# Decode attention on one core: keys and values in loads of head pairs, scores summed by identity matmuls, values on four column strips

## The chip, the cores and the metric

The kernel runs on one core of a Trainium2 chip. The metric is device time in microseconds, the median of several executions. One further execution is taken with the hardware profiler; its own span (first to last instruction) is what the views of the profile divide up.

## The reference

One token (a row of 640 numbers) passes a conditioned transformer block: a modulation from `c`, a layer norm, attention over a cache, a second layer norm, and a gated feed-forward layer. Cut to what matters:

```python
# x: 1 x 640, k_cache and v_cache: 32 heads x 16384 x 128, all bf16
mod = (silu(c) @ w_mod)                      # six vectors of 640: sa, ca, ga, sb, cb, gb
h = layernorm(x) * (1 + ca) + sa
q = (h @ wq)                                 # 32 heads x 128
scores = einsum('hd,hkd->hk', q, k_cache) * 128 ** -0.5
p = softmax(scores)
o = einsum('hk,hkd->hd', p, v_cache)
x = x + ga * (o.reshape(1, 4096) @ wo)
h = layernorm(x) * (1 + cb) + sb
x = x + gb * ((silu(h @ w_gate) * (h @ w_up)) @ w_down)
```

Each head has one query only, so every key and every value is read once and used once. Keys and values are 268.4 MB of the 290.5 MB that the kernel reads.

## The kernel before

The program is a list of operations. Each one names its engine, a position `pos` in time, the operations that it depends on, and a function that issues it. `emit` sorts each engine's operations by position and writes them out one after another, with a semaphore wait in front of an operation where a dependency asks for one. So the order on each engine and on each DMA queue is what the positions say. All large loads are issued from SyncE's queue (SP) in that order; a load that waits holds up those behind it.

The start: `w_mod` (4.9 MB), `w_q` (5.2 MB) and the keys of heads 0 and 1 are issued at once, head 0 in four pieces; `c` and `x` come as columns over the 128 partitions, 10 bytes each, on ScalarE's queue. TensorE makes the modulation and then `q`, every head's row copied onto all partitions (`qbc`, L337).

Then, head by head, with 128 positions of the cache on each of 128 partitions:

- Keys. `kring` has two buffers of one head (32 KB a partition). VectorE multiplies the whole buffer by the query (L414), adds the upper half of each row of 128 to the lower half (L416), folds twice more to 32 and 16 columns (L423), sums the last 16 (L426), and takes the maximum of the 128 scores of each partition (L429).
- Softmax. GpSimd reduces the maximum over the partitions (L432). ScalarE makes the exponentials (L436) with the sum of each partition. GpSimd sums those over the partitions (L439), and ScalarE makes the reciprocal through Ln and Exp (L441, L443).
- Values. `vring` has two buffers of one head. TensorE multiplies them, four positions at a time: the stationary operand is 128 x 4 exponentials, the moving operand 128 x 512 values, 32 matmuls a head, into 4 x 512 of PSUM (L453). ScalarE copies that out (L459), and four fp32 matmuls pick the four diagonal blocks and add them (`diag`, L466). For the last head, whose values come in three pieces, the values are the stationary operand (L477).
- The results are laid out for the output projection (L487 to L496).

The key load of head h + 1 waits for the sum L426 of head h - 1, and the value load of head h waits for the value matmuls of head h - 2; they alternate on SP.

The end: `w_o` is loaded ahead of the last values, `w_gate`, `w_up` and `w_down` follow into the key buffers once these are free. Behind the last values come the projection (L519), a layer norm of six small steps on three engines (L283 to L295), the gate and up matmuls (L562), the down matmuls (L580), and the store.

Of the kernel before, what the change touches and what calls it, by code (L numbers as in the profile page):

```python
# [21 lines left out]
class _Op:  # L22
    __slots__ = ("eng", "pos", "fn", "deps", "chan", "val", "name", "seq", "sig")

    def __init__(self, eng, pos, fn, deps, name, seq, chan=None):
        self.eng = eng
        self.pos = pos
        self.fn = fn
        self.deps = [d for d in deps if d is not None]
        self.name = name  # L30
        self.seq = seq
        self.chan = chan
        self.val = None
        self.sig = False


class _Plan:

    ENGS = ("sp", "act", "dve", "pe", "pool")

    def __init__(self, nc, es):
        self.nc = nc
        self.es = es
        self.ops = []
        self.chans = {}
        for e in self.ENGS:
            if e == "sp":
                continue
            self.chans[e] = _Chan(es.enter_context(nc.semaphore("ch_" + e)), 1)
        self.dma_chans = {}  # L50
        self.names = None
# [7 lines left out]
    def op(self, eng, pos, fn, deps=(), name=""):  # L59
        o = _Op(eng, pos, fn, list(deps), name, len(self.ops))  # L60
        self.ops.append(o)
        return o

    def dma(self, pos, out_ap, in_ap, slot_key, deps=(), name="", eng="sp", noncontig=False):
        nc = self.nc

        def fn(e, out_ap=out_ap, in_ap=in_ap, noncontig=noncontig):
            if noncontig:
                with nc.allow_non_contiguous_dma(reason="tiny vector layout change"):
                    return e.dma_start(out_ap, in_ap)  # L70
            return e.dma_start(out_ap, in_ap)

        o = _Op(eng, pos, fn, list(deps), name, len(self.ops), chan=self.dma_chan(slot_key))
        o.sig = True
        self.ops.append(o)
        return o

    def emit(self, block):
        nc = self.nc
        bad = []  # L80
        for o in self.ops:
            for d in o.deps:
                d.sig = True
                if not ((d.pos, d.seq) < (o.pos, o.seq)):
                    bad.append("%s(%s@%.2f) depends on later %s(%s@%.2f)" % (o.name, o.eng, o.pos, d.name, d.eng, d.pos))
        assert not bad, "plan order violates dependencies:\n" + "\n".join(bad[:40])
        per_eng = {e: [] for e in self.ENGS}
        for o in self.ops:
            per_eng[o.eng].append(o)
        for e in self.ENGS:  # L90
            per_eng[e].sort(key=lambda o: (o.pos, o.seq))
# [6 lines left out]
        self.per_eng = per_eng  # L98

        def run(eng_name, eng):  # L100
            known = {}
            for o in per_eng[eng_name]:
                need = {}
                for d in o.deps:
                    assert d.val is not None, (o.name, d.name)
                    k = id(d.chan)
                    if k not in need or need[k][1] < d.val:
                        need[k] = (d.chan, d.val)
                for k, (ch, v) in need.items():
                    if known.get(k, 0) >= v:  # L110
                        continue
                    eng.wait_ge(ch.sem, v)
                    known[k] = v
                ins = o.fn(eng)
                if ins is not None and self.names is not None:
                    self.names[ins.ins.name] = o.name
                if o.sig:
                    assert ins is not None, o.name
                    ins.then_inc(o.chan.sem, o.chan.inc)
# [21 lines left out]

def build(nc, A_x, A_k, A_v, A_wq, A_wo, B_wg, B_wu, B_wd, c_in, w_mod, out):
# [3 lines left out]
    assert Dh == 128 and D % 128 == 0 and S % 128 == 0  # L146
    KC = D // 128
    TT = S // 128
    NF = F // 128
    FR = F - 128 * NF  # L150
    FCH = NF + (1 if FR else 0)
    GQ = 4

    GROUPS = [(0, 8), (8, 8), (16, 8), (24, 4), (28, 4)]
    assert H % GQ == 0 and all(128 % n == 0 for _, n in GROUPS) and GROUPS[-1][0] + GROUPS[-1][1] == H
    SCALE = float(Dh) ** -0.5
    EPS = 1e-5
    PERIOD = 19.8
    NKP0 = 4

    def TK(h):
        return 20.0 + PERIOD * h

    es = ExitStack()
    with es:
        block = es.enter_context(nc.Block())
        plan = _Plan(nc, es)

        def sb(name, shape, dtype):
            return es.enter_context(nc.sbuf_tensor(name, list(shape), dtype))  # L170

        WM_E = KC * 6 * D
        WQ_E = KC * H * 128
        FFN_E = 2 * KC * F + FCH * D
        VEX = 10240
        wreg = sb("wreg", [128, max(WM_E, H * D)], BF16)
        wm_v = wreg[:, 0:WM_E].rearrange("p (k n) -> p k n", k=KC)
        wo_v = wreg[:, 0:H * D].rearrange("p (k n) -> p k n", k=H)  # L180
        kring = sb("kring", [128, 2, TT, 128], BF16)
        vbig = sb("vbig", [128, 2 * TT * 128 + VEX], BF16)
        vring = vbig[:, 0:2 * TT * 128].rearrange("p (s t d) -> p s t d", s=2, t=TT)
        assert WQ_E - VEX <= TT * 128
        wq_v = vbig[:, 2 * TT * 128 + VEX - WQ_E:2 * TT * 128 + VEX].rearrange("p (k n) -> p k n", k=KC)
        assert FFN_E <= 2 * TT * 128
        kflat = kring[:].rearrange("p s t d -> p (s t d)")
        wg_v = kflat[:, 0:KC * F].rearrange("p (k n) -> p k n", k=KC)
        wu_v = kflat[:, KC * F:2 * KC * F].rearrange("p (k n) -> p k n", k=KC)
        wd_v = kflat[:, 2 * KC * F:2 * KC * F + FCH * D].rearrange("p (k n) -> p k n", k=FCH)  # L190
        acc_sb = sb("acc_sb", [4, 2, 512], F32)
        ident_f = sb("ident_f", [4, 4], F32)
        qbc = sb("qbc", [128, H, 128], BF16)
        S_sb = sb("S_sb", [128, 2, TT], F32)
        P_sb = sb("P_sb", [128, 2, TT], BF16)
        ones_f = sb("ones_f", [128, 128], F32)
        ones_bf = sb("ones_bf", [128, 128], BF16)
        ident = sb("ident", [128, 128], BF16)
        msk = {n: sb("msk%d" % n, [128, 128 // n], F32) for n in sorted({n for _, n in GROUPS})}
        e8 = {n: sb("e%d" % n, [128, n], BF16) for n in sorted({n for _, n in GROUPS})}  # L200
        Z = sb("Z", [128, len(GROUPS), 128], BF16)
        A_sb = sb("A_sb", [128, H], BF16)
        c_col = sb("c_col", [128, KC], BF16)
        x_col = sb("x_col", [128, KC], BF16)
        pm = sb("pm", [128, H], F32)
        gm = sb("gm", [128, H], F32)
        nb = sb("nb", [128, H], F32)
        rs = sb("rs", [128, H], F32)
        Ls = sb("Ls", [128, H], F32)
        lnl = sb("lnl", [128, H], F32)  # L210
        rl = sb("rl", [128, H], F32)
        on_f = sb("on_f", [128, H], F32)
        warm = sb("warm", [128, 2], F32)
# [4 lines left out]
        rr = sb("rr", [128, KC], F32)  # L218
        silu_c = sb("silu_c", [128, KC], BF16)
# [22 lines left out]
        q_ps = [psb[0], psb[1]]  # L242
        OT_ps = psb[2]
        attn_ps = psb[3]
        mod_ps = psb[4]
        A_ps = psb[5]
        st_ps = psb[6]
        f_ps = psb[7]
        acc_ps = [psb[0], psb[1]]
        g_ps = psb[0]  # L250
        u_ps = psb[1]

        POOL, ACT, DVE, PE = "pool", "act", "dve", "pe"
        op = plan.op


        o_onesf = op(DVE, 0.0, lambda e: e.memset(ones_f[:], 1.0), name="ones_f")
        o_ones = op(POOL, 0.0, lambda e: e.memset(ones_bf[:], 1.0), name="ones")
        o_ident = op(POOL, 0.1, lambda e: e.affine_select(
            out=ident[:], in_=ones_bf[:], pattern=[[1, 128]], compare_op=ALU.is_equal,  # L260
            fill=0.0, base=0, channel_multiplier=-1), deps=[o_ones], name="ident")
        o_wz = op(DVE, 0.1, lambda e: e.memset(warm[:], 1.0), name="warm0")
        op(POOL, 0.2, lambda e: e.partition_all_reduce(
            warm[:, 1:2], warm[:, 0:1], channels=128, reduce_op=bass.bass_isa.ReduceOp.max), deps=[o_wz], name="warm")
# [4 lines left out]
        d_c = plan.dma(0.0, c_col[:], c_in[0].rearrange("(p k) -> p k", p=128), "c", name="dma_c", eng="act")  # L269
        d_x = plan.dma(0.01, x_col[:], A_x[0, 0].rearrange("(p k) -> p k", p=128), "x", name="dma_x", eng="act")  # L270
        d_wm = plan.dma(0.0, wm_v, wm_src, "wm", name="dma_wmod")
        d_wq = plan.dma(0.1, wq_v, wq_src, "wq", name="dma_wq")


        op(ACT, 0.05, lambda e: e.preload_act_table_set("natural_log_exp_and_others"), name="tbl")
        o_ec = op(ACT, 0.2, lambda e: e.activation(out=ec[:], in_=c_col[:], func=ACTF.Exp, scale=-1.0), deps=[d_c], name="ec")  # L276
# [360 lines left out]
```

## Time and profile before

| | us |
|---|---|
| Median of the 3 runs | 693.13 (692.8 to 693.34) |
| Span of the profiled execution | 690.5 |
| VectorE busy | 616.9 (89%) |
| GpSimd busy | 381.3 (55%) |
| TensorE busy, matmuls | 361.5 (52%) |
| ScalarE busy | 81.1 (12%) |
| DMA packets of SP's queue, share of 16 engines | 98.4% |
| Mean granted TensorE clock | 0.722 of full speed |

Busy time is the time in which an engine executes an instruction; the share is that of the span. DMA shares are the time of the packets over 16 DMA engines; a packet is one contiguous row, 32 KB for keys and values here. A line such as L414 is line 414 of the kernel. In the list of groups, `out<-in` gives the tiles, then partitions x elements, the count, the busy time, the mean of one, and the idle time in front with what ended it.

### The profile page before, as it was taken

Reading aid. Unit: us, or ns where it says so; the run is one execution under the profiler, and the core shown is the slowest. Engines: PE = TensorE matmul, PEld = TensorE weight load, DVE = VectorE, ACT = ScalarE, POOL = GpSimd, SP = SyncE. Lnnn points to the kernel's source line nnn. Section 1 sums busy time; section 2 is a strip of 40 time slices with the busy share of each in tenths; the row PEclk is TensorE's granted clock in tenths of the full one; section 3 lists DMA queues with packets and bytes.
Section 4 is the critical chain, followed back from the end, with each engine's and each line's share of the span. In section 5 each row is a group of like instructions: output and inputs, shape, how many; then the busy total and the mean of one; then the engine's idle time right before and its main releaser. Section 6 shows DMA issues by size and latency. Waiting matters only on the chain.

```text
span 690.5 us, 4719 instructions
## 1 busy us (share of the span) xinstructions
PE 361.5 (52%) x1940; PEld 159.6 (23%) x1941; DVE 616.9 (89%) x226; ACT 81.1 (12%) x284; POOL 381.3 (55%) x71
## 2 busy tenths in 40 slices
PE   0275055665445455565545445556544544656577
PEld 0242022221112122222112112222111212222176
DVE  0099999999999999999999999999999999999900
ACT  0021001111011111111011110111101111111110
POOL 0005565555777666555677656555577766655500
PEclk9987567667766767767777776766776776676655
DMA  9999999999999999999999999999999999999994
GB/s 382 404 436 400 416 427 427 429 431 433 427 432 433 429 435 426 437 429 432 431 433 427 433 435 429 432 431 431 432 433 427 431 432 435 433 425 430 420 426 177
DMA packets 12150, 290.78 MB, mean 421 GB/s; under 512 B 1696, under 2 KB 1760, under 8 KB 2400
## 3 DMA queue, kind: packets, MB, share of 16 engines
q1 hardware_dynamic: 11840, 290.48, 98.4%
q8 instruction: 15, 0.25, 0.1%
q10 hardware_dynamic: 288, 0.00, 0.0%
q14 instruction: 7, 0.06, 0.0%
HBM read 290.47 MB, written 0.00 MB: 421 GB/s over the span
## 4 chain that ended last, share of the span: by engine, by line
DVE 89%; DMA 7%; PE 2%; issue 1%; ACT 0%; ACTq 0%; DVEq 0%; SPq 0%
DVE kring L414 40%; DVE kring L416 21%; DVE kring L423 16%; DVE S_sb L426 11%; DMA x_col<-in_A_x_dram 4%; DMA kring<-in_B_w_up_dram 3%; DVE pm L429 1%; PE psb L562 1%; PE psb L580 0%; PE psb L311 0%; PE psb L333 0%; ACT qbc L337 0%; PE psb L283 0%; PE psb L290 0%; DVE e L396 0%
## 5 line engine op out<-in xcount | busy, mean ns | idle before, releaser
L453 PE MATMUL psb<-vbig,P_sb 128*4 128x512 bf16 x992 | 286.8, 460 | 263.3 <-ACT P_sb L436 244.9
L432 POOL PARTITION_ALL_REDUCE gm<-pm x32 | 262.3, 8198 | 226.7 <-DVE pm L429 226.7
L414 DVE TENSOR_TENSOR kring<-kring,qbc 128x16384 bf16<-128x16384 bf16 (+1 forms) x35 | 278.3, 7950 | 3.2 <-ACT qbc L337 3.2
L453 PEld LDWEIGHTS psb<-vbig,P_sb 128*4 128x4 bf16 x992 | 94.8, 98 | 442.2 <-ACT P_sb L436 265.9
L416 DVE TENSOR_TENSOR kring<-kring 128x8192 bf16<-128x8192 bf16 (+1 forms) x35 | 142.1, 4059 | 1.2
L439 POOL PARTITION_ALL_REDUCE Ls<-rs x32 | 117.9, 3683 | 29.7 <-ACT P_sb L436 29.7
L423 DVE TENSOR_TENSOR kring<-kring 128x4096 bf16<-128x4096 bf16 x64 | 112.5, 1758 | 2.2
L426 DVE TENSOR_REDUCE S_sb<-kring 128x128 f32<-128x2048 bf16 x32 | 73.1, 2286 | 1.1
L466 PE MATMUL psb<-ident_f,acc_sb 4*128 4x1 f32 x248 | 32.5, 248 | 23.8 <-ACT acc_sb L459 23.8
L459 ACT ACTIVATE acc_sb<-psb,rl 4x512 f32<-4x512 f32 x31 | 21.0, 678 | 155.4 <-PE psb L453 155.3
L466 PEld LDWEIGHTS psb<-ident_f,acc_sb 4*128 4x128 f32 x248 | 29.8, 186 | 39.5 <-ACT acc_sb L459 39.5
L434 ACT ACTIVATE nb<-gm 128x1 f32<-128x1 f32 x32 | 6.5, 202 | 222.7 <-POOL gm L432 222.7
L441 ACT ACTIVATE lnl<-Ls 128x1 f32<-128x1 f32 x32 | 6.5, 203 | 121.8 <-POOL Ls L439 121.8
L283 PE MATMUL psb<-st,ones_f 128*128 128x1 f32 x4 | 1.2, 362 | 29.0 <-ACT x_f L300 28.4
L540 DVE TENSOR_TENSOR tt<-attn_bf,modb 128x5 f32<-128x5 bf16 x1 | 0.2, 166 | 14.7 <-ACT attn_bf L539 14.7
L277 DVE TENSOR_SCALAR dd<-ec 128x5 f32<-128x5 f32 x1 | 0.2, 172 | 14.7 <-ACT ec L276 14.7
L436 ACT ACTIVATE P_sb<-S_sb,nb 128x128 bf16<-128x128 f32 x32 | 12.9, 402 | 1.2
L285 DVE SCALAR_TENSOR_TENSOR xc<-x_f,psb 128x5 f32<-128x5 f32 x1 | 0.2, 161 | 12.6 <-PE psb L283 12.6
L333 PE MATMUL psb<-vbig,h_col 128*128 128x512 bf16 x39 | 10.4, 434 | 0.9 <-DVE h_col L319 0.9
L429 DVE TENSOR_REDUCE pm<-S_sb 128x1 f32<-128x128 f32 x32 | 9.2, 286 | 1.1
L490 ACT ACTIVATE Z<-msk,on_f 128x16 bf16<-128x16 f32 (+1 forms) x32 | 10.0, 311 | 1.1
L562 PE MATMUL psb<-h_col,kring 128*128 128x1 bf16 (+1 forms) x140 | 8.8, 199 | 1.2 <-DVE h_col L549 1.0
(63 smaller groups left out, 91.2 us busy)
## 6 DMA issues: line engine op xcount, KB each, us to landing
kring<-in_A_k_cache_dram SPq DMA_DIRECT2D x31, 4096.0 KB, 16.5
vbig<-in_A_v_cache_dram SPq DMA_DIRECT2D x31, 4096.0 KB, 25.7
vbig<-in_A_wq_dram SPq DMA_DIRECT2D x1, 5120.0 KB, 26.6
wreg<-in_w_mod_dram SPq DMA_DIRECT2D x1, 4800.0 KB, 14.5
kring<-in_A_k_cache_dram SPq DMA_DIRECT2D x4, 1024.0 KB, 31.5
wreg<-in_A_wo_dram SPq DMA_DIRECT2D x1, 3840.0 KB, 37.7
kring<-in_B_w_gate_dram SPq DMA_DIRECT2D x1, 2160.0 KB, 18.5
kring<-in_B_w_up_dram SPq DMA_DIRECT2D x1, 2160.0 KB, 23.8
```

The lines of the kernel that those rows point to most:

```text
L414: o_m = op(DVE, base + 3.3 * c, lambda e, ksl=ksl, qb=qb: e.tensor_tensor(out=ksl, in0=ksl, in1=qb, op=ALU.mult), deps=[d_k[h][c], o_qbc[h ...
L416: fd.append(op(DVE, base + 3.3 * c + 2.2 + (6.6 if npc == 1 else 0.0), lambda e, ksl=ksl: e.tensor_tensor(out=ksl[:, :, 0:64], in0=ksl[:, ...
L423: prev = [op(DVE, base + 15.5 + 1.5 * i, lambda e, kslot=kslot, w=w: e.tensor_tensor(out=kslot[:, :, 0:w], in0=kslot[:, :, 0:w], in1=kslot ...
L426: o_red[h] = op(DVE, base + 18.2, lambda e, s2=s2, kslot=kslot, w=w: e.tensor_reduce(out=S_sb[:, s2], in_=kslot[:, :, 0:w], axis=AX.X, op= ...
L429: o_max = op(DVE, base + 18.5, lambda e, h=h, s2=s2: e.tensor_reduce(out=pm[:, h:h + 1], in_=S_sb[:, s2], axis=AX.X, op=ALU.max), deps=[o_ ...
L432: o_gm = op(POOL, base + 19.0, lambda e, h=h: e.partition_all_reduce(gm[:, h:h + 1], pm[:, h:h + 1], channels=128, reduce_op=bass.bass_isa ...
L436: o_exp[h] = op(ACT, base + 19.4, lambda e, h=h, s2=s2: e.activation(out=P_sb[:, s2], in_=S_sb[:, s2], func=ACTF.Exp, scale=SCALE, bias=nb ...
L439: o_L = op(POOL, base + 20.0, lambda e, h=h: e.partition_all_reduce(Ls[:, h:h + 1], rs[:, h:h + 1], channels=128, reduce_op=bass.bass_isa. ...
L453: last = e.matmul(acc_ps[s2][0:4, :], lhsT=P_sb[:, s2, 4 * c:4 * c + 4], rhs=vring[:, s2, 4 * c:4 * c + 4, :].rearrange("p t d -> p (t d)" ...
L459: o_acc[h] = op(ACT, base + 28.6, lambda e, h=h, s2=s2: e.activation(out=acc_sb[:, s2], in_=acc_ps[s2][0:4, :], func=ACTF.Copy, scale=rl[0 ...
L466: last = e.matmul(OT_ps[:, h:h + 1], lhsT=acc_sb[:, s2, 128 * i:128 * (i + 1)], rhs=ident_f[:, i:i + 1], start=(i == 0), stop=(i == 3))
L562: last = e.matmul(ps_t[0:w, j:j + 1], lhsT=wv[:, k, cols], rhs=h2_col[:, k:k + 1], start=(k == 0), stop=(k == KC - 1))
```

## The change

The body is rewritten. What changes in what is done:

- Two heads are worked on together, 64 partitions each. A load brings the keys (or values) of a pair: 8.39 MB, 256 positions or 64 KB contiguous on each partition. Keys have two buffers of a pair; values have one buffer of a pair, so the values of pair p wait for the value matmuls of pair p - 1.
- VectorE multiplies by the query and folds once, from 128 columns to 64, in two halves (32 of the 64 remaining columns each). The remaining sum of 64 is made on TensorE: 64 matmuls with the identity as the stationary operand accumulate in PSUM; the moving operand takes one column of all 256 positions, a step of 128 elements.
- The maximum over the partitions of a head: VectorE takes each partition's maximum from PSUM, ScalarE spreads it over a diagonal, a matmul with a block matrix of ones brings all of a head's values to each of its partitions, and VectorE takes the minimum (signs are turned). The sums of the exponentials are added up once, at the end, by one matmul.
- The values of a pair are 64 matmuls of 512 columns with 128 x 8 exponentials (those of the other head are zero); they go to four column strips of the array in turn, each with its own 32 partitions of PSUM.
- On TensorE the order in step p is: first half of the sums, values of pair p - 1, second half of the sums, `diag` of pair p - 1, the matmul of the maximum.
- `w_mod` lies in the second key buffer at first, `w_q` in the value buffer, `w_o` comes into the first key buffer ahead of the last values, the feed-forward weights into the second. `c` and `x` come as rows and are turned by matmuls. The chunks of the feed-forward layer are taken with a step of four columns, `w_up` comes in two parts.
- Operations have no position any more; each engine runs them in the order in which they are listed. The planner can write a loop, but `LOOP_ON` is empty, so all is written out.

```diff
-        kring = sb("kring", [128, 2, TT, 128], BF16)
-        vbig = sb("vbig", [128, 2 * TT * 128 + VEX], BF16)
+        kring = sb("kring", [128, 2, T2, 128], BF16)
+        vbuf = sb("vbuf", [128, T2, 128], BF16)
...
-        kv = lambda t, h: t[0, h].rearrange("(p t) d -> p t d", p=128)
+        k_src = lambda p: A_k[0, 2 * p:2 * p + 2].rearrange("h (q t) d -> (h q) t d", q=64)
+        v_src = lambda p: A_v[0, 2 * p:2 * p + 2].rearrange("h (q t) d -> (h q) t d", q=64)
...
+        def load_k(p):
+            deps = [o_R[p - 2]] if p >= 2 else ([o_mod] if p == 1 else [])
+            d_k[p] = dma(kring[:, p % 2], k_src(p), ("k", p % 2), deps=deps, name="dma_k%d" % p)
+
+        def load_v(p):
+            deps = [o_pv[p - 1]] if p >= 1 else [o_q[-1]]
+            cuts = VCUT if p == NP - 1 else [0, T2]
+            d_v[p] = [dma(vbuf[:, a:b, :], v_src(p)[:, a:b, :], ("v", c), deps=deps, name="dma_v%d_%d" % (p, c))
+                      for c, (a, b) in enumerate(zip(cuts, cuts[1:]))]
+
+        def pv(p):
...
+                    for j in range(a // 4, b // 4):
+                        s = j % 4
+                        last = e.matmul(acc_ps[32 * s:32 * s + 8, :], lhsT=PZ[:, p % 2, j, :],
+                                        rhs=vbuf[:, 4 * j:4 * j + 4, :].rearrange("p t d -> p (t d)"),
+                                        start=(j < 4), stop=(j >= NCH - 4), tile_position=(0, 32 * s))
...
+        def diag(p):
+            def f_diag(e):
+                last = None
+                for i in range(4):
+                    last = e.matmul(OT_ps[:, 0:2], lhsT=acc_sb[:, 128 * i:128 * (i + 1)], rhs=sel[:, i:8:4],
+                                    start=(i == 0), stop=(i == 3))
...
+        def reduce_mm(p, c, fold):
+            def f_R(e):
+                last = None
+                for d in range(QW * c, QW * c + QW):
+                    last = e.matmul(S_ps[p % 2][:, 0:T2], lhsT=ident[:], rhs=kring[:, p % 2, :, d],
+                                    start=(d == 0), stop=(d == 63))
+                return last
...
+        def fold(p, c):
+            kv4 = kring[:, p % 2].rearrange("p t (a d) -> p t a d", a=2)[:, :, :, QW * c:QW * c + QW]
...
+            o_m = op(DVE, lambda e: e.tensor_tensor(out=kv4, in0=kv4, in1=q4, op=ALU.mult),
+                     deps=[d_k[p]] + o_qev[p // 2], name="mult%d_%d" % (p, c))
+            return op(DVE, lambda e: e.tensor_tensor(out=kv4[:, :, 0], in0=kv4[:, :, 0], in1=kv4[:, :, 1], op=ALU.add),
+                      deps=[o_m], name="fold%d_%d" % (p, c))
+
+        def step(p):
+            f0 = fold(p, 0)
+            r0 = reduce_mm(p, 0, f0)
+            if p >= 1:
+                pv(p - 1)
+            f1 = fold(p, 1)
+            o_R[p] = reduce_mm(p, 1, f1)
+            if p >= 1:
+                diag(p - 1)
+            o_pm = op(DVE, lambda e: e.tensor_reduce(
+                out=pm[:, p:p + 1], in_=S_ps[p % 2][:, 0:T2], axis=AX.X, op=ALU.max), deps=[o_R[p]], name="pm%d" % p)
+            o_d2 = op(ACT, lambda e: e.activation(out=d2[:], in_=negid[:], func=ACTF.Copy, scale=pm[:, p:p + 1]),
+                      deps=[o_pm, o_negid], name="d2_%d" % p)
+            o_mx = op(PE, lambda e: e.matmul(mx_ps[:, 0:64], lhsT=bd_f[:], rhs=d2[:], start=True, stop=True),
...
+            o_nb[p] = op(DVE, lambda e: e.tensor_reduce(
+                out=nb[:, p:p + 1], in_=mx_ps[:, 0:64], axis=AX.X, op=ALU.min), deps=[o_mx], name="nb%d" % p)
...
         load_k(0)
         load_k(1)
+        load_v(0)
+        step(0)
+        load_k(2)
+        step(1)
+        load_v(1)
...
+        for p in range(2, NP):
+            plan.in_loop(LOOP_ON, "pairs", (p - 2) // 2, NLOOP)
+            if p + 1 < NP:
+                load_k(p + 1)
...
+            step(p)
+            load_v(p)
```

## The prediction

> **What bounds the kernel now.** I read the page's slices and chain first, then how long each key load takes to land, then the instruction groups, then the first 75 and the last 60 us of the timeline. Slices and chain:
>
> ```profile
> DVE  0099999999999999999999999999999999999900
> ...
> DMA  9999999999999999999999999999999999999994
> ...
> DVE 89%; DMA 7%; PE 2%; issue 1%; ACT 0%; ACTq 0%; DVEq 0%; SPq 0%
> ```
>
> VectorE and the DMA engines are both full from slice 2 to 38; the chain names VectorE because it never waits. Whether the DMA has anything to spare shows in the time from issue to landing of the key load of one head, near 110 us and near 616 us (two answers of the DMA view, a line of each):
>
> ```profile
> kring<-in_A_k_cache_dram SPq DMA_DIRECT2D x1, 4096.0 KB, 13.2
> ```
>
> ```profile
> kring<-in_A_k_cache_dram SPq DMA_DIRECT2D x1, 4096.0 KB, 19.6
> ```
>
> It is issued when VectorE frees its buffer, once per head; 6.4 us more over some 26 heads means that a head's 8.39 MB takes about 0.25 us longer than VectorE's 19.28 us (start to start of L414 in the chain, 596.73 to 616.01). So the DMA is the slower of the two, at about 19.5 us a head, and VectorE lives off a shrinking lead. Whatever VectorE is spared, the steady part cannot get shorter than the bytes. The groups (busy, mean ns, idle before):
>
> ```profile
> L453 PE MATMUL psb<-vbig,P_sb 128*4 128x512 bf16 x992 | 286.8, 460 | 263.3 <-ACT P_sb L436 244.9 <-DMA vbig<-in_A_v_cache_dram 18.4
> L414 DVE TENSOR_TENSOR kring<-kring,qbc 128x16384 bf16<-128x16384 bf16 x31 | 269.1, 8681 | 0.0
> L416 DVE TENSOR_TENSOR kring<-kring 128x8192 bf16<-128x8192 bf16 x31 | 137.2, 4425 | 1.1
> L423 DVE TENSOR_TENSOR kring<-kring 128x4096 bf16<-128x4096 bf16 x32 | 73.3, 2292 | 1.1
> L426 DVE TENSOR_REDUCE S_sb<-kring 128x128 f32<-128x2048 bf16 x32 | 73.1, 2286 | 1.1
> ```
>
> TensorE's pace is read from one burst of 32 value matmuls cut in two (busy and count, granted clock, DMA share, GB/s):
>
> ```profile
> 57.70:60.60 2.90, 2.90 (x7) 0.50 0.84 362
> 60.60:66.00 5.40, 5.40 (x26) 1.00 1.06 452
> ```
>
> A burst starts at half clock, 0.42 us per 512 columns, and goes on at 0.21. Over all heads (286.8 us / 31 = 9.25 us a burst) some 11 of 32 run cold, 4.8 us. The end of the kernel:
>
> ```profile
> 667.36 1.01 PE L477 MATMUL psb<-P_sb,vbig 128*128 128x1 bf16 x32 [1.42 <-DMA vbig<-in_A_v_cache_dram]
> ...
> 673.98 4.42 PE L562 MATMUL psb<-h_col,kring 128*128 128x1 bf16 x70 [1.05 <-DVE h_col L549]
> ...
> 678.59 4.40 PE L562 MATMUL psb<-h_col,kring 128*128 128x1 bf16 x70 [0.19 <-DMA kring<-in_B_w_up_dram]
> ...
> 683.33 3.12 PE L580 MATMUL psb<-gu_col,kring 64*128 64x1 bf16 x60 [0.34 <-DVE gu_col L571]
> ```
>
> The last values land at 667.3, and 23.2 us of single-file work follow to 690.5. So the time is: when the last value bytes land, plus that tail. I cost the change in these two terms.
>
> **VectorE and TensorE per pair of heads.** Removed: two folds at L423 (2.29 and 1.23 us), the sum at L426 (2.29) and the maximum per head, and all GpSimd reductions (L432, L439). Left: per half of a pair one multiply of 16,384 (8.68) and one fold of 8,192 (4.43): 13.1 us, 26.2 a pair against 38.6. The runs are 32 long instead of 128; the folds with runs of 64, 32 and 16 all cost 0.16 us over 1.92 elements per ns, so the run length is free. Added on TensorE: 64 matmuls of 256 columns (R, two halves of 32), reading one element in every 256 B. No row has such a moving operand. By columns alone a half costs 32 x 0.21 = 6.8 us at half clock and 3.5 at full. Nearest rows for a stride: weight loads with a one-column matmul at clock 0.50, 31 ns contiguous (L477), 52 with a step of 10 B (L580, 70 in 3.8 us), 63 with 26 B (L562). That is 126 ns per 256 strided elements, under the 213 of a cold matmul (no loss); taken as a ratio it doubles a half, to 13.6 us. I take 6.8: the bursts start after 7 us or more of idle TensorE, hence cold, and the nearest count stays under it.
>
> The Trainium skill ("SBUF — State Buffer", Specifications) speaks against this: lines are 16 bytes, and full bandwidth needs at least two hits in each; R has one. It gives no factor; L580 and L562 agree in direction (52 and 63 ns).
>
> Values: 64 matmuls of 512 columns a pair, on four column strips. Bounds: all four at once, 16 x 0.216 = 3.5 us; one after another, 13.8 (both warm, since R's first half runs just ahead). No row has two strips. I take 3.5, because the strips share neither array columns nor PSUM partitions, and L477 issues a matmul every 31 ns, so 64 of them need only 2.0 us of issue. The skill ("TensorE: Matmul & The Clock Gate", Part 3) reports 2.38x for three strips; with 3x it would be 4.6 us and the sum 1.1 later.
>
> The softmax step waits on TensorE: VectorE's maximum of 256 from PSUM (0.4, from 0.29 for 128), a scale on ScalarE (0.2), an fp32 matmul (0.7, from 0.59 at L283), a minimum (0.2), hand-overs: 1.8 us; with the four `diag` matmuls (1.05, L466) and their copy queued ahead, 2.7. VectorE idles through R's second half and this, its next multiply standing behind `nb`. A pair takes 26.2 + 6.8 + 2.7 = 35.7 us, with R's first half and the values (10.3) under the second multiply and fold (13.1). The DMA needs 38.8. So the steady part stays the DMA's: nothing gained or lost but its bytes' pace, and 3 us a pair of cover.
>
> **Descriptors.** Packets in the trace: 8 KB 309 ns, 32 KB 1,215, 40 KB 1,514: about 8 ns fixed each. A 64-KB row saves one, and a semaphore write per load goes: 8 x 8 + 9 = 73 ns for each of 32 loads, -2.3 us. Bounds: 0 if rows are cut in two; a loss is unlikely, as rate rises with size (26.5, 27.0, 27.1 B/ns).
>
> **Head of the kernel.** The key load after the start found the queue empty before, 13.3 us to land instead of 9.7 (first line of the DMA view of 55.5 to 56.5 us); that gap and the next one cost 2.0 us. After: w_q lands at 27.8 as now; key pair 0 19.4 later, 47.2 (VectorE starts 11.6 us later than its 35.7 now, covered by its shorter pairs). Keys 1, values 0, keys 2, values 1 could follow without a gap until 124.8. But with one value buffer, values 1 wait for pv of pair 0, which stands on TensorE behind R's first half of pair 1: 47.3 + 26.2 + 6.8 + 1.8 = 82.1, + 13.1 + 6.8 + 3.5 = 105.5 to issue, + 19.4 + 3.6 (empty queue) = 128.5. Gap 3.8, so +1.8. Bounds: at 3.5 a half no gap, -2.0; at 13.6, +15.5. Later value loads wait the same way but are issued some 6 us before the queue empties (pair 2: about 140 against 146). The key loads stand in front of them on SP and wait for R of two pairs earlier, which is done first. In the last pair w_o is put ahead of the last values and covers their wait by 6 us.
>
> **Tail.** Last quarter of the last values, 16 matmuls: 0.9 to 1.8 against 1.05. Then, against 1.1 us from values to w_o now: a copy from PSUM (0.7), `diag` 1.1, three VectorE or ScalarE steps and one matmul (1.1): +1.9. Gate and up read weights 8 B apart instead of 26: 70 x 52 ns instead of 63, -0.8 each, and up no longer waits 0.2. Sum +0.6, from 0 to +1.5. Gone from the chip altogether: GpSimd's 381 us, off the path, worth nothing.
>
> **Sum.** 690.5 - 2.3 + 1.8 + 0.6 = 690.6. The runs shown have a median 2.6 above the profiled span, so 693.2: no change (a difference under 0.2%, 1.4 us, can't be told from none).
>
> **Rivals.**
> 1. *The head gap closes*: R warm from the start (3.5 a half). 690.5 - 2.3 - 2.0 + 0.3 = 686.5, 689 measured. For: the clock turned in 2.9 us in the burst shown. Against: 4.8 on average, and 7 us of idle ahead.
> 2. *Strided reads bind* (slower). With every element at half the full rate a half is 0.42 x 11 + 0.21 x 21 = 9.3 us: head gap 8.8, 695.6, 698 measured, the pair at 38.2 still hidden. This is the place where the skill's line rule would bite. From 9.8 us a half (306 ns a matmul) the pair passes 38.8 and every pair pays: at 13.6 a pair is 13.1 + 13.6 + 3.5 + 13.6 + 2.7 = 46.5, 7.7 x 14 pairs more, near 800. For: 63 against 31 ns. Against: both are below what a matmul of 256 needs.
> 3. *Strips run one after another* (13.8): values 1 issued 10.3 later in the head; pairs at 13.1 + 6.8 + 13.8 + 3.5 + 2.7 = 39.9, barely over; pv of pair 14 outruns w_o's cover by 7; last quarter +3. 690.6 + 20 = 711, 713 measured. For: nothing in the trace overlaps two matmuls. Against: the disjoint strips.
> 4. *64-KB rows are cut in two*: +2.3, 695.5; inside the forecast's range. A loop cannot slip in: `LOOP_ON` is empty.
>
> **How the numbers follow.** Forecast 0.48, its own range 689.5 to 697; rival 1 0.17, rival 2 0.22 (half of it above 705), rival 3 0.13. Faster: rival 1 and 0.13 of the forecast, 0.30. Same 0.17. Slower: 0.18 of the forecast with rivals 2 and 3, 0.53. The range 689 to 714 leaves out the worst of rival 2.
>
> **What would show it.** R's halves at 5.8 to 6.8 us and clock 0.5 to 1.0 in them; value bursts of 3.5 to 5; VectorE waiting for key loads from pair 4 on, 26.2 busy of 38.8; 64-KB packets near 2,420 ns; values 1 landing at 127 to 129 us; the last values near 665 to 668 and 23.5 to 24.5 us behind them. Wrong if VectorE waits for TensorE in the middle pairs, or if the loads stand idle there.

## The result and the profile after

The changed kernel takes 870.73 us (median of 4 runs, 869.71 to 871.27) against 693.1 for the kernel before (4 runs on the same chip): a ratio of 1.2561, with a 95% interval of 1.2543 to 1.2579. The prediction was 693.2 us with a range of 689 to 714. The profiled execution has a span of 869.2 us, against 690.5 before, and a mean granted TensorE clock of 0.585, against 0.722.

The slices of the changed kernel (busy tenths in 40 slices of the span; `PEclk` is the granted clock) and the first line of its chain of waits:

```profile
DVE  1083836539091745729092654819183562909211
...
PEclk9955565555656565565656565565656555565655
DMA  9998939597894959598694959689594959777492
...
PE 68%; DVE 25%; DMA 5%; ACT 1%; issue 1%; SPq 0%; DVEq 0%
```

Neither VectorE nor the DMA is full any more, and the chain runs through TensorE for 68% of the time (2% before). The DMA view of 300 to 400 us, in 2.5-us slices, shows what became of the resource that bounded the kernel before. Twice it stands still for four slices, some 10 us:

```profile
DMA  9999000099999999999999990000999999999999
```

The groups (busy, mean ns of one | idle before and what ended it):

```profile
L471 PE MATMUL psb<-kring,ident 128*128 128x256 bf16 x1024 | 445.9, 607 | 222.8 <-DVE kring L481 222.8
L479 DVE TENSOR_TENSOR kring<-kring,qbc 128x16384 bf16<-128x16384 bf16 x32 | 277.9, 8683 | 25.4 <-DMA kring<-in_A_k_cache_dram 25.4
...
L493 DVE TENSOR_REDUCE pm<-psb 128x1 f32<-128x256 f32 x16 | 6.8, 425 | 319.1 <-PE psb L471 319.1
L481 DVE TENSOR_TENSOR kring<-kring 128x8192 bf16<-128x8192 bf16 x32 | 141.6, 4425 | 1.1
L444 PE MATMUL psb<-vbuf,PZ 128*8 128x512 bf16 x1024 | 89.3, 523 | 0.3 <-PE psb L444 0.3
```

VectorE's instructions cost what was forecast (8.68 and 4.43 us), but it idles 319 us in front of L493, the maximum, waiting for the sums at L471. Those are 445.9 us in 1,024 matmuls: 0.435 us each (1,024 times the mean of 607 ns would be 622 us, so the records of neighbours overlap; busy time over count is the pace). The forecast had 6.8 us for 32, which is 0.21. One pair in the timeline (start, length, what it is):

```profile
400.06 8.69 DVE L479 TENSOR_TENSOR kring<-kring,qbc 128x16384 bf16<-128x16384 bf16 x1
400.20 13.92 PE L471 MATMUL psb<-kring,ident 128*128 128x256 bf16 x32 [13.38 <-DVE kring L481]
...
414.06 5.00 PE L444 MATMUL psb<-vbuf,PZ 128*8 128x512 bf16 x64
418.99 13.95 PE L471 MATMUL psb<-kring,ident 128*128 128x256 bf16 x32
432.97 0.42 DVE L493 TENSOR_REDUCE pm<-psb 128x1 f32<-128x256 f32 x1 [19.76 <-PE psb L471]
...
435.94 8.68 DVE L479 TENSOR_TENSOR kring<-kring,qbc 128x16384 bf16<-128x16384 bf16 x1
```

Read from the multiply of the pair's first half, which starts at 387.01: 13.05 us to the first fold's end, 13.9 of sums, 5.0 of values, 13.9 of sums, 3.0 for the softmax step, and the next pair starts 48.93 us after this one. The DMA needs 38.8 and waits for the rest. Granted clock of the same sums and values, in windows (width, TensorE busy and count, clock, DMA share, GB/s; the lines of two answers, sums first):

```profile
400.20:404.00 3.80, 3.80 (x9) 0.50 1.25 539
404.00:414.05 10.05, 10.05 (x24) 0.50 0.50 215
419.00:422.00 3.00, 3.00 (x8) 1.00 0.99 350
422.00:426.00 4.00, 4.00 (x11) 0.71 1.17 508
426.00:432.90 6.90, 6.90 (x17) 0.50 0.90 389
```

```profile
414.05:416.80 2.75, 2.74 (x28) 0.50 0.00 0
416.80:419.00 2.20, 2.20 (x40) 0.98 0.00 0
```

The first half of the sums runs 13.9 us without a break and never gets the full clock. The second starts with it, inherited from the value matmuls, and loses it while it runs. It makes no difference to the sums: 13.92 against 13.95 us, about 0.4 us each in every window.

Where the 178.7 us of span went is best seen against a kernel that is bound by its bytes, the first experiment below (687.8 us). The times at which value loads land give (values 1 is the value load of pair 1; pairs count from 0): values 1 at 143.9 against 126.1 us (17.8 later), then 13 pairs to values 14 at 49.5 against 38.9 us each (138.0), and from there to the end 81.2 against 55.6 (25.6). That is 181.4 in all.

### The profile page after: what moved, and what is told of

It is laid out like the page before. It is cut to its first block, busy times and chain, and to the rows that moved or that the text cites. A ratio compares the mean times of both kernels' runs of the same rounds, so it can differ in the third digit from the quotient of the medians.

```text
span 869.2 us, 6001 instructions
## 1 busy us (share of the span) xinstructions
PE 604.5 (70%) x2793; PEld 216.2 (25%) x2793; DVE 435.7 (50%) x142; ACT 45.8 (5%) x145; POOL 0.7 (0%) x6
## 4 chain that ended last, share of the span: by engine, by line
PE 68%; DVE 25%; DMA 5%; ACT 1%; issue 1%; SPq 0%; DVEq 0%
PE psb L471 51%; DVE kring L479 16%; PE psb L444 10%; DVE kring L481 8%; DMA kring<-in_A_k_cache_dram 5%; PE psb L459 3%; PE psb L497 1%; PE psb L603 1%; PE psb L647 1%; ACT d L495 1%; PE psb L668 0%; ACT OT_sb L464 0%; DVE nb L499 0%; ACT PZ L503 0%; PE psb L588 0%
## 5 line engine op out<-in xcount | busy, mean ns | idle before, releaser
L471 PE MATMUL psb<-kring,ident 128*128 128x256 bf16 x1024 | 445.9, 607 | 222.8 <-DVE kring L481 222.8
L479 DVE TENSOR_TENSOR kring<-kring,qbc 128x16384 bf16<-128x16384 bf16 x32 | 277.9, 8683 | 25.4 <-DMA kring<-in_A_k_cache_dram 25.4
L471 PEld LDWEIGHTS psb<-kring,ident 128*128 128x128 bf16 x1024 | 121.2, 121 | 529.1 <-issue 302.7
L493 DVE TENSOR_REDUCE pm<-psb 128x1 f32<-128x256 f32 x16 | 6.8, 425 | 319.1 <-PE psb L471 319.1
L481 DVE TENSOR_TENSOR kring<-kring 128x8192 bf16<-128x8192 bf16 x32 | 141.6, 4425 | 1.1
L444 PE MATMUL psb<-vbuf,PZ 128*8 128x512 bf16 x1024 | 89.3, 523 | 0.3 <-PE psb L444 0.3
L444 PEld LDWEIGHTS psb<-vbuf,PZ 128*8 128x8 bf16 x1024 | 28.6, 109 | 65.5 <-issue 56.6
L459 PEld LDWEIGHTS psb<-sel,acc_sb 128*128 128x128 f32 x128 | 29.5, 319 | 7.6 <-issue 4.6
L459 PE MATMUL psb<-sel,acc_sb 128*128 128x2 f32 x128 | 26.2, 327 | 0.7 <-ACT acc_sb L450 0.7
L497 PE MATMUL psb<-d,bd_f 128*128 128x64 f32 x32 | 11.0, 448 | 10.4 <-ACT d L495 10.4
L503 ACT ACTIVATE PZ<-psb,nb 64x256 bf16<-64x256 f32 x32 | 15.0, 469 | 16.8 <-DVE nb L499 16.6
L407 PE MATMUL psb<-vbuf,h_col 128*128 128x512 bf16 x40 | 10.4, 426 | 6.9 <-DMA vbuf<-in_A_wq_dram 6.9
L495 ACT ACTIVATE d<-negid,pm 128x64 f32<-128x64 f32 x16 | 5.6, 348 | 49.9 <-DVE pm L493 49.6
L617 DVE TENSOR_TENSOR on_f<-psb,rl 128x2 f32<-128x2 f32 x1 | 0.2, 159 | 14.6 <-PE psb L459 14.6
```

What stands on the lines that cost most here:

```text
L407: last = e.matmul(q_ps[b][:, 0:512], lhsT=h_col[:, k:k + 1].broadcast_to([128, 128]), rhs=wq_v[:, k, g * 512:(g + 1) * 512], start=(k == 0 ...
L444: last = e.matmul(acc_ps[32 * s:32 * s + 8, :], lhsT=PZ[:, p % 2, j, :], rhs=vbuf[:, 4 * j:4 * j + 4, :].rearrange("p t d -> p (t d)"), st ...
L459: last = e.matmul(OT_ps[:, 0:2], lhsT=acc_sb[:, 128 * i:128 * (i + 1)], rhs=sel[:, i:8:4], start=(i == 0), stop=(i == 3))
L471: last = e.matmul(S_ps[p % 2][:, 0:T2], lhsT=ident[:], rhs=kring[:, p % 2, :, d], start=(d == 0), stop=(d == 63))
L479: o_m = op(DVE, lambda e: e.tensor_tensor(out=kv4, in0=kv4, in1=q4, op=ALU.mult), deps=[d_k[p]] + o_qev[p // 2], name="mult%d_%d" % (p, c))
L481: return op(DVE, lambda e: e.tensor_tensor(out=kv4[:, :, 0], in0=kv4[:, :, 0], in1=kv4[:, :, 1], op=ALU.add), deps=[o_m], name="fold%d_%d" ...
```

## The experiments

The theory: a matmul whose moving operand takes one element in 256 B runs at a quarter of the full rate, and everything else of the change is near its forecast. The rivals: the shape is at fault (the wait between engines, the single value buffer, the strips, whatever the operand); or the reads are slow because VectorE and the DMA use the same memory at the time.

### The same sums from a contiguous constant

Each sum reads one contiguous tile of 256 columns instead of the products, so the scores, and all that follows, are not the reference's; every wait and every other instruction is kept.

```diff
-    last = e.matmul(S_ps[p % 2][:, 0:T2], lhsT=ident[:], rhs=kring[:, p % 2, :, d],
+    last = e.matmul(S_ps[p % 2][:, 0:T2], lhsT=ident[:], rhs=kconst[:],
```

(In this kernel and in all those below with runs of four or two, the tile `rows`, used only at the start, lies in the unused end of the value buffer, for space.)

> The 64 sums read a constant tile of 256 adjacent columns in place of every 128th column of the keys (scores and output are then not the reference's); all else, waits and order too, as in the changed kernel. Theory 'stride' (a moving operand with each element in a line of its own is what costs 0.43 us a matmul): a matmul falls to 0.11 to 0.21 us, a half to 3.5 to 6.8, and the rest of the prediction's sum holds: span 688 to 694. Rival 'shape' (256 columns behind a reloaded 128 x 128 identity cost 0.43 us in any case): unchanged, 870. Rival 'contention' (VectorE or the DMA writing into the same buffer slows the read): also fast here, and told apart by the run of steps.

Measured: 690.29 us, ratio to before 0.9962 (0.9945 to 0.9979). The span is 687.8 us. Three of its groups:

```profile
L481 DVE TENSOR_TENSOR kring<-kring,qbc 128x16384 bf16<-128x16384 bf16 x32 | 278.0, 8687 | 90.3 <-DMA kring<-in_A_k_cache_dram 90.3
L473 PE MATMUL psb<-kconst,ident 128*128 128x256 bf16 x1024 | 172.3, 349 | 344.8 <-DVE kring L483 344.8
...
L495 DVE TENSOR_REDUCE pm<-psb 128x1 f32<-128x256 f32 x16 | 6.8, 425 | 82.5 <-PE psb L473 82.5
```

The sums fall from 445.9 to 172.3 us, 5.4 a half. VectorE waits 82.5 us for the sums (L495), against 319.1, and 90.3 for key loads, against 25.4; the chain of waits runs through loads for 62% of the time and through TensorE for 11%. One operand carries the whole loss, and not the shape of the change. That it is the operand's address pattern, and not its values (the constant is zero) or its place, is left to the runs below.

### The step by itself

A kernel with no attention and nothing beside TensorE: 32 matmuls of 256 columns with one access pattern, 40 contiguous ones to bring the clock up, the next pattern, and so on. The moving operands alone, some left out:

```diff
+ rhs=flat[:, 0:256]      rhs=flat[:, 0:512:2]    rhs=flat[:, 0:1024:4]   rhs=flat[:, 0:2048:8]
+ rhs=flat[:, 0:32768:128]    rhs=big[:, 0:128, 0:2]    rhs=big[:, 0:64, 0:4]
```

> No attention: groups of 32 matmuls of 256 columns with a 128 x 128 stationary operand, each group with another step between moving columns (1 to 128 elements) or with runs of 2 to 32 adjacent columns and 128 elements between runs, with 40 adjacent-column matmuls of 512 between the groups; nothing else runs. 'Stride': 0.43 us at a step of 128 with nothing beside it, at full and at half clock; 0.11 (full clock) at a step of 1; steps up to 4 elements (8 B) little dearer, from 8 elements (16 B) the whole price; runs of 2 half of it, runs of 4 and more near none. 'Contention': 0.11 to 0.21 at every step. 'Shape': 0.43 at step 1 too.

Measured, in the groups (L224 contiguous, L230 step 2, L236 step 4, L242 step 8, L266 step 128, L272 runs of two adjacent elements 128 apart, L278 runs of four):

```profile
L242 PE MATMUL ps<-big,one 128*128 128x256 bf16 x32 | 14.6, 630 | 0.0
...
L266 PE MATMUL ps<-big,one 128*128 128x256 bf16 x32 | 14.0, 609 | 0.0
...
L236 PE MATMUL ps<-big,one 128*128 128x256 bf16 x32 | 7.4, 405 | 0.0
L272 PE MATMUL ps<-big,one 128*128 128x256 bf16 x32 | 7.1, 392 | 0.0
...
L230 PE MATMUL ps<-big,one 128*128 128x256 bf16 x32 | 3.8, 275 | 0.0
...
L278 PE MATMUL ps<-big,one 128*128 128x256 bf16 x32 | 3.7, 270 | 0.0
...
L224 PE MATMUL ps<-big,one 128*128 128x256 bf16 x32 | 3.7, 273 | 0.0
```

With nothing beside it, step 128 costs 14.0 us for 32, as in the kernel. So contention falls. The price is not in the distance, for 8 is no cheaper than 128, nor in jumping, for runs of four are as cheap as contiguous. It counts how many elements of each 16 bytes (8 bf16) are used: one costs 0.436 us a matmul at step 128 (0.46 at step 8), two 0.22 to 0.23, four or more the full rate, 0.115. That is about 1.7 ns for each 16-byte line visited. The lines named are those of the Trainium skill ("SBUF — State Buffer", Specifications), and its direction is confirmed; but by its two hits in a line step 4 should have run at full rate, and it took twice the time, so here the measurement decides. The expectation missed the same point: it had steps up to 4 little dearer than adjacent columns.

The clock in the step-8 group (window columns as before):

```profile
89.70:94.00 4.30, 4.30 (x10) 1.00 0.00 0
94.00:104.20 10.20, 10.20 (x23) 0.50 0.00 0
```

It begins at full clock and drops to half some 4.4 us in, although TensorE is never idle, and the pace stays.

### Lines or steps

Steps that are no power of two, and runs that begin at other elements, tell "lines visited" from "elements a step apart". No attention here either; the moving operands alone, some left out:

```diff
+ rhs=flat[:, 0:768:3]    rhs=flat[:, 0:1280:5]   rhs=flat[:, 0:1536:6]
+ rhs=big[:, 0:64, 2:6]   rhs=big[:, 0:64, 4:8]   rhs=big[:, 0:64, 6:10]   rhs=big[:, 0:128, 6:8]   rhs=big[:, 0:128, 7:9]
```

> As the run of steps (no attention, groups of 32 matmuls of 256 columns), with steps of 1, 3, 5, 6 and 12 elements, and runs of 2, 4 or 8 adjacent columns every 128 elements that start at other places in a 16-byte line. Theory 'price per 16-byte line, 1.7 ns': steps of 3, 5, 6 and 12 elements meet 96, 160, 192 and 256 lines: 0.16, 0.27, 0.33 and 0.43 us; runs of 4 that start at element 2 or 4 stay at 0.11, from element 6 they straddle two lines: 0.22; runs of 2 at element 6 0.22, at 7 (two lines) 0.43; runs of 8 from element 4: 0.11. Rival 'price per 8-byte piece': runs of 4 from element 2 already double, steps of 3 to 6 elements dearer than this.

Measured (L224 step 3, L230 step 5, L236 step 6, L248 runs of four from element 2, L254 runs of four from element 4, L260 runs of four from element 6, L266 runs of two from element 6, L272 runs of two from element 7):

```profile
L272 PE MATMUL ps<-big,one 128*128 128x256 bf16 x32 | 14.0, 609 | 0.0
...
L236 PE MATMUL ps<-big,one 128*128 128x256 bf16 x32 | 11.0, 518 | 0.0
L230 PE MATMUL ps<-big,one 128*128 128x256 bf16 x32 | 9.2, 462 | 0.0
L260 PE MATMUL ps<-big,one 128*128 128x256 bf16 x32 | 7.1, 396 | 0.0
L266 PE MATMUL ps<-big,one 128*128 128x256 bf16 x32 | 7.1, 392 | 0.0
L224 PE MATMUL ps<-big,one 128*128 128x256 bf16 x32 | 5.7, 336 | 0.0
...
L248 PE MATMUL ps<-big,one 128*128 128x256 bf16 x32 | 3.7, 270 | 0.0
L254 PE MATMUL ps<-big,one 128*128 128x256 bf16 x32 | 3.7, 270 | 0.0
```

The same run of two costs 7.1 us inside a line and 14.0 across the border of two; the same run of four, 3.7 inside and 7.1 across. Only the alignment differs. Runs of four from element 2 (L248), which lie in one line but in two pieces of 8 bytes, cost 3.7, so the rival falls. Steps 3, 5 and 6 visit 96, 160 and 192 lines for 256 elements: at 1.70 ns that is 5.2, 8.7 and 10.4 us for 32, and 5.7, 9.2 and 11.0 were measured. So the price counts lines, and these steps cost 6 to 9% more than that.

### The real sums in runs of four, and of two

This kernel computes all of the reference. A matmul takes four adjacent columns of 128 positions, 512 elements in 128 lines; 16 make a half. VectorE then adds the four partial sums of each position from PSUM.

```diff
-    for d in range(QW * c, QW * c + QW):
-        last = e.matmul(S_ps[p % 2][:, 0:T2], lhsT=ident[:], rhs=kring[:, p % 2, :, d], ...
+    for d in range(QW * c, QW * c + QW, RW):                     # RW = 4
+        for b in range(NBK):                                     # NBK = 2, TB = 128
+            last = e.matmul(S_ps[b][:, :], lhsT=ident[:], rhs=kring[:, p % 2, TB * b:TB * b + TB, d:d + RW], ...
...
+    e.tensor_reduce(out=S_sb[:, TB * b:TB * b + TB],
+                    in_=S_ps[b][:, :].rearrange("p (t w) -> p t w", w=RW), axis=AX.X, op=ALU.add)
```

> The sums read runs of 4 adjacent columns of 128 positions, 512 columns a matmul, 16 matmuls a half; VectorE adds the 4 partial sums of each score from PSUM (two sums of 512, about 0.7 us each) before the maximum. 'Stride' with a price per line: a matmul needs 128 lines x 1.68 ns = 0.215 us, no more than 512 columns need anyway; a half 4 to 6.8 us; a pair 26.2 + 6.8 + 1.4 + 2.7 = 37.1, under the DMA's 38.8; span 690 to 695. 'Shape' (a price per matmul): 16 x 0.43 = 6.9 a half, 690 to 695 as well. A price per element with a step anywhere in the pattern: 0.86 us a matmul, 870 to 890.

Measured: 690.24 us, ratio 0.9963 (0.9949 to 0.9977), span 686.6. Two of its groups and the value matmuls in its timeline:

```profile
L485 DVE TENSOR_TENSOR kring<-kring,qbc 128x16384 bf16<-128x16384 bf16 x32 | 278.0, 8686 | 79.1 <-DMA kring<-in_A_k_cache_dram 79.1
L477 PE MATMUL psb<-kring,ident 128*128 128x512 bf16 x512 | 174.9, 514 | 333.9 <-DVE kring L487 333.9
```

```profile
399.18 3.63 PE L449 MATMUL psb<-vbuf,PZ 128*8 128x512 bf16 x64 [0.91 <-DMA vbuf<-in_A_v_cache_dram]
```

The sums of the same products, in the same place and in another order of reading, take 174.9 us instead of 445.9, and the 180 us are gone. It also shows the values: 64 matmuls of 512 columns in 3.63 us.

Runs of two (`RW = 2`, everything else the same):

> As the run with 4 adjacent columns, but with 2 adjacent columns of all 256 positions, 512 columns a matmul, 16 matmuls a half, one sum of 512 on VectorE (0.7 us). Price per line: 256 x 1.68 = 0.43 us a matmul at either clock, a half 6.9 us, a pair 26.2 + 6.9 + 0.7 + 2.7 = 36.5; span 689 to 694. Price per element: 0.86 us a matmul, near 870.

Measured: 691.62 us, ratio 0.9981 (0.9972 to 0.999), span 689.0. The sums cost 225.6 us in 512 matmuls, 7.05 a half. That is near the 6.8 that the prediction took, for another reason, and the kernel then comes out as it had said, 1.6 us under the predicted time.

### Half the strided sums, and a second fold

The step of 128 is kept, and a second fold on VectorE (2.29 us) halves the number of sums.

```diff
-    for d in range(QW * c, QW * c + QW):
+    for d in range(QW * c, QW * c + QW // 2):
...
+    lo, hi = (kring[:, p % 2, :, QW * c + x:QW * c + x + QW // 2] for x in (0, QW // 2))
+    return op(DVE, lambda e: e.tensor_tensor(out=lo, in0=lo, in1=hi, op=ALU.add), deps=[o_f], ...
```

> The changed kernel with a second fold on VectorE (2.29 us a half) and so 16 strided sums a half instead of 32. Theory 'stride, on the path': a half of the sums 16 x 0.43 = 6.9 us; a pair 2 x 15.4 + 6.9 + 3.0 = 40.7; pair 1 starts at 47.3 + 30.8 + 6.9 + 1.8 = 86.8, 15 pairs to 697.3 less 3.0, the changed kernel's 40.3 from its last sum to the end: span 734.6, measured near 736. Rival (the sums slow VectorE or the loads in some other way than by their own length): well over 750.

Measured: 740.2 us, ratio 1.0675 (1.066 to 1.0691), span 739.2. In its timeline:

```profile
389.75 8.68 DVE L479 TENSOR_TENSOR kring<-kring,qbc 128x16384 bf16<-128x16384 bf16 x1
389.89 7.04 PE L471 MATMUL psb<-kring,ident 128*128 128x256 bf16 x16 [15.70 <-DVE kring L484]
396.86 4.70 PE L444 MATMUL psb<-vbuf,PZ 128*8 128x512 bf16 x64
...
430.72 8.68 DVE L479 TENSOR_TENSOR kring<-kring,qbc 128x16384 bf16<-128x16384 bf16 x1
```

Half the sums take half the time, 7.04 us, and a pair takes 40.97 (from 389.75 to 430.72). A half of about 7 us does not by itself spare the kernel: runs of two had the same, but there no second fold lay in front of it. With 15.4 of VectorE a half the pair is 30.8 + 7.1 + 3.0 = 40.9, over the DMA's 38.7, and every pair pays. The time is 4 us above the 736 expected: a pair takes 0.25 us more than the 40.7 of that sum, in each of 15 pairs.

### The strips

The kernel with runs of four, all values on one strip of the array.

```diff
-    last = e.matmul(acc_ps[32 * s:32 * s + 8, :], ..., start=(j < 4), stop=(j >= NCH - 4), tile_position=(0, 32 * s))
+    last = e.matmul(acc_ps[0:8, :], ..., start=(j == 0), stop=(j == NCH - 1))
```

> The kernel with runs of 4, all value matmuls on one column strip. If the strips ran side by side before: values take 13.8 us or a little more instead of 3.6, a pair 13.1 + 5.3 + 13.8 + 4 to 5.3 + 3.2 = 39.4 to 40.7 against the DMA's 38.7, some 10 us in the head, some 8 at the end: 715 to 745. If the strips did not matter: 690.

Measured: 721.71 us, ratio 1.0404 (1.039 to 1.0417), span 720.2. In its timeline:

```profile
416.38 13.98 PE L449 MATMUL psb<-vbuf,PZ 128*8 128x512 bf16 x64
...
430.28 3.63 PE L477 MATMUL psb<-kring,ident 128*128 128x512 bf16 x16
```

13.98 us on one strip against 3.63 on four: a factor of 3.9, the four run at once. The Trainium skill ("TensorE: Matmul & The Clock Gate", Part 3) gives 2.38x for three strips; four are worth more here. Against runs of four on four strips, values 1 land 11.2 us later (139.2 against 128.05), the 13 pairs after them take 7.9 more, and what follows values 14 takes 14.6 more: the head, the pairs just over the bytes, and an uncovered end, as the third rival had them, though it had 10.3, nothing and 10 for the three.

### 64-KB rows cut in two

The kernel with runs of four, each pair's load made as two loads with rows of 32 KB (the keys' edit; that of the values is alike, and the value matmuls wait for both halves).

```diff
-    d_k[p] = dma(kring[:, p % 2], k_src(p), ...)
+    d_k[p] = [dma(kring[:, p % 2, a:a + T2 // 2, :], k_src(p)[:, a:a + T2 // 2, :], ...) for a in (0, T2 // 2)]
```

> The kernel with runs of 4, each pair's load cut into two loads with rows of 32 KB, waits unchanged. Theory 'fixed time per packet': 38.86 us between loads of a pair instead of 38.70, 2.4 us over 15 pairs: 692.6. Rival (row length is free here): 690.2.

Measured: 693.68 us, ratio 1.0004 (0.9995 to 1.0012), 3.4 us above the same kernel with whole rows. That one ran on another chip; by the two ratios to the kernel before, each taken on its own chip, the loss is 0.41%, 2.8 us, where 2.4 were expected. From values 1 to values 14 a pair takes 38.97 us against 38.82: 0.15 for two loads, 75 ns each, where the prediction had worked out 73. The 64-KB packets are not cut: 3,968 of them in the changed kernel, median 2,419 ns, against 1,215 for 32 KB.

### The best version

The kernel with runs of four, and in step 1 the values of pair 0 ahead of the first half of the sums on TensorE, so that the load of values 1 is issued before the queue runs empty.

```diff
     f0 = fold(p, 0)
+    if p == 1:
+        pv(0)
     r0 = reduce_mm(p, 0, f0)
-    if p >= 1:
+    if p >= 2:
         pv(p - 1)
```

> The kernel with runs of 4, and in step 1 alone the values of pair 0 stand ahead of the first half of the sums on TensorE. Theory 'head gap' (values 1 are issued late and the DMA engines idle, and nothing later gives that back): values 1 land near 125 instead of 128.1 us, all later loads 3.1 earlier; 690.2 - 3.1 = 687.1. Rival (the gap is taken up by slack behind it): 690.2, unchanged.

Measured: 687.89 us, ratio 0.9915 (0.99 to 0.9929), so 0.85% under the kernel before. By the two ratios that is 3.3 us less than with runs of four, where 3.1 were expected. Values 1 land at 125.7 us instead of 128.05. It beats both kernels, and what is left is bytes: a key load still ends VectorE's wait in the middle of the kernel.

```profile
416.75 8.69 DVE L485 TENSOR_TENSOR kring<-kring,qbc 128x16384 bf16<-128x16384 bf16 x1 [4.93 <-DMA kring<-in_A_k_cache_dram]
```

## Why the prediction was wrong

**The step that failed.** The one on the sums: "I take 6.8: the bursts start after 7 us or more of idle TensorE, hence cold, and the nearest count stays under it." A half took 13.9 us. Two things in that sentence fell. First, the clock does not price a strided sum: 13.92 us at clock 0.50 and 13.95 from 1.00 down. Secondly, the argument by the nearest count compared 126 ns of strided weight load with the 213 ns of a cold matmul as if the larger would cover the smaller. The rows L477, L580 and L562 were of weight loads, another operand, and of steps of 10 and 26 B; read as a ratio they gave the upper bound of 13.6, which was right to 0.3 us. That is luck: the ratio of 2 belongs to weight loads at half clock and was laid on the pace of a cold matmul, while the measured price is the same at both clocks and is 3.8 times the full rate (0.436 against 0.115 us). The bound was written down and had no chance beyond its part in rival 2, though the sentence beside it, on one hit in each line, spoke for it as well.

**The rival that came true.** "Strided reads bind" had the mechanism, a threshold (9.8 us a half; no run lies between 7.1 and 13.9, so it is not tested) and the price at the bound (46.5 a pair, near 800). It was put at 0.22, half of that above 705, and the range left its worst case out. Put together from its parts, 128.5 to values 1, 14 pairs of 46.5 and 23.8 behind the last values, that price is 803 us of span; 869 were measured, and the 66 us lie in three places. A pair took 49.5 us in the mean, not 46.5 (42 us over 14 pairs): 0.6 for the two halves of sums at 13.9; 2.1 for the values, 5.0 and 6.1 in turn instead of 3.5, since sums at half clock no longer leave the array warm for them; 0.3 in the softmax step. The delay in the head, +15.5 in the prediction's own bounds, was not added to it: values 1 came at 143.9 us, 15.4 late, where that bound means 142.3. And behind the last values, which land at 837.1, there are 32.1 us, 8.3 more than the 23.8: TensorE comes to them only at 841.6, because the sums (to 828.9), the softmax step and 140 matmuls of the projection stand ahead of them.

**What held,** as the other runs show:

- The steady part is the DMA's: 38.9 us a pair by the landings in the kernel with a constant operand, 38.8 forecast. VectorE's half: 13.05 and 13.1.
- Values on four strips: 3.63 us warm, 3.5 forecast; on one strip 13.98, 13.8 forecast.
- The softmax wait: 3.0 (in the changed kernel) and 2.7. The descriptors: 75 ns a load and 73.
- The head: values 1 at 128.05 us with runs of four (halves of 5.3 to 6.2 us there, and VectorE's addition of 1.3) and at 130.2 with runs of two (7.05 and 0.7), 128.5 forecast for halves of 6.8 and no addition. Where the value matmuls of pair 0 went first, the gap closed.
- The tail: 23.7 us behind the last values with the constant operand (664.1 to 687.8), 21.9 and 22.1 with runs of four and two, 23.9 in the best version; 23.8 forecast.
- The sum of 690.6: spans of 686.6 to 689.0 in the three versions whose halves take 5.4 to 7.1 us. It was 1.6 to 4 us high, part of which is the tail just named, and part that sums that start cold warm up on the way (6.1 to 6.4 us a half there, with the constant operand), so that the head's gap was smaller than 3.8 (values 1 at 126.1).

So one size, of one term, out of a sum whose other terms came out near their forecast once this one did, moved the time by 180 us. It could, because this term stands twice on the chain of a pair, with VectorE waiting for the second: 3 us of cover, then every microsecond of a half counts twice in each pair.

## What to carry to other kernels

Before a sum is put on TensorE, count the 16-byte lines that its moving operand visits: where each line gives fewer than four bf16 elements, price the matmul at no less than 1.7 ns a line, whether the granted clock is 0.50 or 1.00. If the layout cannot change, take four adjacent columns that lie in one line in one matmul, and add the four partial results later; here that cost 1.3 us of VectorE a pair and saved 17 of TensorE. And where the only rows for an unseen operation lie far from it, give the dearer end a weight of its own and price it through to the head and the end of the kernel.

## What was not expected of the hardware

- The price of a strided moving operand is in time, not in clock cycles of the array: 13.9 us at clock 0.50 and at a clock falling from 1.00.
- The granted clock falls, or does not rise, under strided matmuls that keep TensorE busy without a gap: in the groups with one element a line from 1.00 to 0.50 some 3 to 6 us in, and 0.50 throughout the first half of the sums in the kernel. The groups of steps 4 and 5, 7.4 and 9.2 us long, kept 1.00. The kernel's mean is 0.585 with 604.5 us of busy TensorE, and 0.704 with 289.8 in the version with a constant operand.
- Steps of 8 and 16 elements cost 14.6 and 14.9 us for 32 matmuls, steps of 32 to 128 cost 13.9 to 14.0, though all visit one line for each element. Why is open.
